# A halved bank, halved merges and stores in the last block, and a new order of all work, in an attention-plus-gated-FFN kernel

## The chip, the core and the metric

The kernel runs on one core of one Trainium2 chip. The metric is the device time of one execution in microseconds (us), lower is better. A core has TensorE (PE: matmuls, with its weight loads listed apart as PEld), VectorE (DVE), ScalarE (ACT), GpSimd (POOL) and SyncE (SP); each of them works through its own list of instructions in order, and they meet through semaphores. Matmuls write into PSUM, which is used here as eight banks of 128 partitions by 512 fp32 numbers; everything else lives in SBUF. DMAs are issued by POOL (all loads) and by SP (transposes and stores).

## The reference

Two layers follow each other. First comes attention with projected keys and values, for 8 batches, 8 heads, 1024 positions and head size 64:

```
k_proj = einsum('ks,bhsd->bhkd', E, k);  v_proj = einsum('ks,bhsd->bhkd', F, v)     # 1024 -> 64
scores = (q @ k_proj^T) / 8;  attn = softmax(scores)
x = (attn @ v_proj), heads side by side, as 8192 tokens of 512
```

Then a gated feed-forward layer, 512 to 1536 and back to 512:

```
out = (sigmoid(x @ w_gate) * (x @ w_val)) @ w_out          # fp32, 8192 x 512
```

## The kernel before

**Blocks.** Each batch has two blocks of 512 tokens, so there are 16 blocks. In a block, three groups of hidden columns are made from x by w_gate and w_val, gated (`tanh` on ACT, `hidden` on DVE), kept as `hT`, and multiplied by w_out. Attention for the next batch runs between the blocks of the present one. Its steps are `kv` (projection), `sc` (scores), `top`, `sub`, `exp` (softmax), `turnp` (a DMA transpose), `xo` (attn times v), `inv`, `ko`, `div` (normalisation) and `turnx` (a DMA transpose to x).

**Seven products.** Apart from block 0, each of the three weight products is done in 2x2 quarters by seven quarter products and not by eight. The sums of quarters that this needs are made in SBUF (`xs`, `s_sum`, `w_sum`, `o_sum`, most through line 547), and the results are put together through three PSUM banks called a, c and f. In the output product (`o_jobs`) bank a gathers A11·B11, S2·T2, A21·T3 and A22·T4. ACT copies it to bank c after the first (`copyO`) and snaps it to SBUF buffers u2 and u3 after the second and third (`snapO`, half scale). Bank c adds A12·B21 and leaves as one quarter of the output (`leaveO`, ACT). Bank f is the shared sum: it takes S1·T1, and DVE merges it with u3 into the quarter (second tokens, second columns); then A12·B22 is added to it, and DVE merges it with u2 into the quarter (first tokens, second columns). A merge is one `scalar_tensor_tensor` of 128x512 (line 1361). The quarter left over comes from bank a at its end. A21 and A12 are overwritten in place by sums; the fourth sum (`sum4`) makes the A12 of the last product.

A quarter product covers 256 tokens, in two halves j of 128 tokens, and writes half j of the bank with 6 matmuls of 128x256. So each half is a job on PE, and a merge waits until both halves are in.

**Stores.** `ost` holds a block's output as four tiles tt of 128 tokens by 512 columns. A quarter is two of those tiles by 256 columns. When both columns' quarters of a tile are there, SP stores the tile (`store`, line 1259, 256 KB), four stores in a block.

**Order.** Nothing schedules at run time. The program first lists all jobs (2911), and then puts them down in the order of the tuple `ORDER`, which so decides the order on every engine at once. `PLACES` says which of the eight banks or thirteen buffers each temporary gets. Waits are derived from the keys that jobs read and write; a bank is one key, so PE's next write into any part of it waits for the readers of all of it. Entries -2 and -1 in `ORDER` are fillers: matmuls of the identity, 512 or 256 columns wide, into bank 7, whose result nobody reads (`busy`). There are 28, all in the first 23 us, while the first inputs land. Then follow the first batch in finer steps (`pk`, `tk`, `tq`, `sc`, `sub`, `pv`, `tp`, `xo0`) and block 0 with plain products (`plainG`, `plainV`).

Of the kernel before, what the change touches and what calls it, by code (L numbers as in the profile page):

```python
# [153 lines left out]
class Job:  # L154
# [222 lines left out]
def bass_linformer_attn__then__ffn_glu_sigmoid_kernel(  # L377
# [11 lines left out]
    B = q.shape[0]  # L389
# [4 lines left out]
    H6 = NF // 2  # L394
# [3 lines left out]
    with contextlib.ExitStack() as es:  # L398
# [103 lines left out]
        def new_bank(**kw):  # L502
            return Slot("bank", group[0], **kw)
# [1373 lines left out]
```

## Time and profile before

| | us |
|---|---|
| median of 3 runs (517.55 to 518.54) | 518.04 |
| the profiled execution | 517.57 |
| its span, first to last instruction | 515.6 |
| last matmul ends, from the span's start | 511.57 |
| PE busy | 509.4 (99%) |
| DVE busy | 443.7 (86%) |
| ACT busy | 371.5 (72%) |
| POOL busy | 173.2 (34%) |

The prediction takes durations from the one profiled execution. Places in time are counted from its span's start. A row of a group is: line, engine, operation, output <- inputs, form, count, then busy time, mean of one in ns, and idle time before. In the timeline a row is: start, length, engine, line, operation, operands, form, count. A matmul's length contains its way through the array, so rows on PE overlap; how densely PE works is read from the distance between starts, which for a 256-column matmul in steady work is 109 ns and for 512 columns 215 ns. The clock granted to TensorE was full throughout (1.000).

### The profile page before, as it was taken

Reading aid. Unit: us, or ns where it says so; the run is one execution under the profiler, and the core shown is the slowest. Engines: PE = TensorE matmul, PEld = TensorE weight load, DVE = VectorE, ACT = ScalarE, POOL = GpSimd, SP = SyncE. Lnnn points to the kernel's source line nnn. Section 1 sums busy time; section 2 is a strip of 40 time slices with the busy share of each in tenths; the row PEclk is TensorE's granted clock in tenths of the full one; section 3 lists DMA queues with packets and bytes.
Section 4 is the critical chain, followed back from the end, with each engine's and each line's share of the span. In section 5 each row is a group of like instructions: output and inputs, shape, how many; then the busy total and the mean of one; then the engine's idle time right before and its main releaser. Section 6 shows DMA issues by size and latency. Waiting matters only on the chain.

```text
span 515.6 us, 12673 instructions
## 1 busy us (share of the span) xinstructions
PE 509.4 (99%) x4975; PEld 420.6 (82%) x4978; DVE 443.7 (86%) x856; ACT 371.5 (72%) x714; POOL 173.2 (34%) x200
## 2 busy tenths in 40 slices
PE   8999999999999999999999999999999999999996
PEld 4556858888888888887888888888888878888885
DVE  6779998499987997889997998989988899977993
ACT  1556866878788587857977777786888669677762
POOL 9975003702435024240354206341163301440020
PEclk9999999999999999999999999999999999999999
DMA  9999958899888248993699937989467953341004
GB/s 167 197 198 207 179 101 181 120 180 223 135 172 147 52 135 123 216 158 88 127 192 183 166 73 143 180 149 139 129 122 175 165 114 76 69 123 61 24 1 164
DMA packets 140411, 71.60 MB, mean 139 GB/s; under 512 B 97216, under 2 KB 132032, under 8 KB 140352
## 3 DMA queue, kind: packets, MB, share of 16 engines
q0 software_dynamic: 35936, 29.89, 38.6%
q1 hardware_dynamic: 104416, 40.91, 37.9%
q8 instruction: 39, 0.64, 0.5%
q14 instruction: 20, 0.16, 0.1%
HBM read 60.29 MB, written 16.78 MB: 149 GB/s over the span
## 4 chain that ended last, share of the span: by engine, by line
PE 96%; DVE 3%; ACT 0%; issue 0%; DVEq 0%
PE pA L518 49%; PE pF L518 47%; DVE topf L1589 1%; DVE hT L1173 1%; DVE spare L1104 0%; DVE pF L1616 0%; DVE pA L1616 0%; DVE hT L547 0%; ACT spare L532 0%; DVE ost L1361 0%; DVE inv L1681 0%; ACT EFT L532 0%; ACT eT L532 0%; DVE KVs L1698 0%; DVE warm L646 0%
## 5 line engine op out<-in xcount | busy, mean ns | idle before, releaser
L532 ACT ACTIVATE spare<-pF 128x512 f32<-128x512 f32 (+2 forms) x157 | 87.4, 574 | 34.9 <-PE pF L518 23.4
L532 ACT ACTIVATE spare<-pA 128x512 f32<-128x512 f32 (+2 forms) x160 | 90.8, 583 | 26.7 <-PE pA L518 18.1
L547 POOL TENSOR_TENSOR hT<-hT,hS 128x512 bf16<-128x512 bf16 x42 | 48.2, 1161 | 131.5 <-PE pA L518 76.5
L1698 POOL TENSOR_TENSOR KVs<-spare,inv 128x256 bf16<-128x256 f32 (+1 forms) x48 | 34.7, 731 | 66.8 <-ACT spare L532 18.4
L1173 DVE SCALAR_TENSOR_TENSOR hT<-spare,pA 128x512 bf16<-128x512 f32 x65 | 43.7, 679 | 10.2 <-PE pF L518 6.1
L532 ACT ACTIVATE spare<-spare 128x512 f32<-128x512 f32 x79 | 48.2, 628 | 5.5 <-DVE spare L1104 5.2
L1104 DVE TENSOR_TENSOR spare<-pA,spare 128x512 f32<-128x512 f32 x62 | 42.0, 682 | 9.6 <-PE pF L518 4.2
L518 PE MATMUL pF<-wO,hT 128*128 128x256 bf16 (+1 forms) x321 | 46.9, 288 | 0.2
L1104 DVE TENSOR_TENSOR spare<-pF,spare 128x512 f32<-128x512 f32 x57 | 38.5, 681 | 3.8 <-PE pF L518 2.1
L1173 DVE SCALAR_TENSOR_TENSOR hT<-spare,pF 128x512 bf16<-128x512 f32 x53 | 35.9, 679 | 4.9 <-PE pF L518 3.4
L518 PEld LDWEIGHTS pF<-wO,hT 128*128 128x128 bf16 x324 | 31.2, 98 | 8.2 <-ACT pF L532 0.2
L518 PE MATMUL pA<-xT,wG 128*128 128x256 bf16 (+1 forms) x216 | 35.1, 284 | 0.0
L518 PE MATMUL pA<-wO,hT 128*128 128x256 bf16 x264 | 34.4, 273 | 0.0
L518 PE MATMUL pA<-xT,wV 128*128 128x256 bf16 (+1 forms) x212 | 34.4, 285 | 0.0
L518 PE MATMUL pA<-wT,hT 128*128 128x256 bf16 x240 | 32.3, 273 | 0.0
L518 PE MATMUL pF<-xT,wV 128*128 128x256 bf16 (+1 forms) x196 | 32.1, 286 | 0.0
L518 PE MATMUL pF<-xT,wG 128*128 128x256 bf16 (+1 forms) x192 | 31.5, 286 | 0.0
L518 PE MATMUL pF<-xS,tV 128*128 128x256 bf16 x200 | 30.0, 273 | 0.0
L518 PEld LDWEIGHTS pA<-wO,hT 128*128 128x128 bf16 x264 | 25.4, 98 | 3.2 <-issue 0.2
L547 POOL TENSOR_TENSOR xS<-xT,xS 128x512 bf16<-128x512 bf16 x14 | 16.9, 1207 | 32.5 <-DVE xS L547 27.5
L518 PE MATMUL pA<-xS,wV 128*128 128x256 bf16 x184 | 27.6, 273 | 0.0
L518 PE MATMUL pA<-xS,tG 128*128 128x256 bf16 x184 | 27.6, 272 | 0.0
(185 smaller groups left out, 1305.7 us busy)
## 6 DMA issues: line engine op xcount, KB each, us to landing
out_dram<-ost SPq DMA_DIRECT2D x64, 256.0 KB, 2.5
KVs<-in_v_dram POOLq DMA_DIRECT2D x15, 512.0 KB, 9.8
KVs<-in_k_dram POOLq DMA_DIRECT2D x14, 512.0 KB, 8.5
Qb<-in_q_dram POOLq DMA_DIRECT2D x14, 512.0 KB, 7.9
wO<-in_moe_w_out_dram POOLq DMA_DIRECT2D x1, 1536.0 KB, 16.6
KVs<-in_k_dram POOLq DMA_DIRECT2D x4, 256.0 KB, 6.2
Qb<-in_q_dram POOLq DMA_DIRECT2D x4, 256.0 KB, 9.5
wG<-in_moe_w_gate_dram POOLq DMA_DIRECT2D x4, 256.0 KB, 11.5
```

The costliest lines, as they stand in the source:

```text
L518: lambda e: e.matmul(o, lhsT, rhs, **kw),
L532: lambda e: e.activation(o, i, func, scale=scale),
L547: fn = lambda e: e.tensor_tensor(o, a, b, op)
L1104: lambda e: e.tensor_tensor(PB(b)[:, :] if stay else BF(s), PB(b)[:, :], BF(s), ALU.add),
L1173: lambda e: e.scalar_tensor_tensor(o, y.rearrange("p (j c) -> p j c", j=2), 1.0, x.rearrange("p (j c) -> p j c", j=2), ALU.add, ALU.mult,),
L1589: lambda e: e.tensor_reduce((top if by_pe(b, t, y) else topf)[:, n : n + 8], PB(bk)[:, :].rearrange("p (n k) -> p n k", n=8), mybir.AxisLi ...
L1698: fn = lambda e: e.tensor_tensor(xto.rearrange("p (g h d) -> p h g d", g=2, h=H)[:, hh[0] : hh[1], :, :], o[:, :, 0:DH].rearrange("p (h g) ...
```

## The change

Three things change together.

1. In the output product of the last block alone, the shared sum f gets a bank for each half j, each started and closed on its own (`own`). The two merges become two each, 128x256, and each waits for its half.
2. The last block's four stores of 256 KB become eight of 128 KB (`store_half`), one for each tile and half of its columns, each of which waits for its own quarter (or half merge).
3. `ORDER` and `PLACES` are new for the whole program, with 2917 jobs, 907 temporaries and 26 fillers (20 of 512 columns, 6 of 256) in place of 2911, 906 and 28 (25 and 3). All other work is the same, instruction for instruction; only its order, its banks and its buffers differ.

```diff
 ORDER = (
-    16, -2, -2, -2, 17, 18, 0, 19, -2, -2, -2, -1, 30, 20, 31, 2, 28, 21, 29, 4, -2, -2, -2, -2, -1, 32, 38, 1,
...
-        def o_product(blk, bk, A, B, j, start=False, stop=False):
+        def o_product(blk, bk, A, B, j, start=False, stop=False, own=False):
...
-                    start=start and m == 0 and j == 0,
-                    stop=stop and m == H6 - 1 and j == 1,
+                    start=start and m == 0 and (own or j == 0),
+                    stop=stop and m == H6 - 1 and (own or j == 1),
...
+        def store_half(blk, tt, col):
+            t = 2 * (2 * (blk % 2) + tt % 2) + tt // 2
+            cc = slice(256 * col, 256 * col + 256)
+            add(
+                "SP",
+                lambda e: e.dma_start(out_v[blk // 2, t][:, cc], ost[:, tt, cc]),
+                r=[("ost", tt, col)],
+                dma=f"out{tt}",
+                cost=0.4,
+                nbytes=128 << 10,
+            )
...
-            a, c, f = new_bank(), new_bank(clean=True), new_bank()
+            last = blk == 2 * B - 1
+            a, c = new_bank(), new_bank(clean=True)
+            f = [new_bank(), new_bank()] if last else [new_bank()] * 2
...
-                        lambda j=j: o_product(blk, b, A, B, j, **kw),
+                        lambda j=j: o_product(blk, b[j] if b is f else b, A, B, j, own=last and b is f, **kw),
...
-                            o,
-                            PB(f)[:, :].rearrange("p (j c) -> p j c", j=2),
+                            o[:, jj, :],
+                            PB(f[jj.start])[:, k].rearrange("p (j c) -> p j c", c=256),
                             0.5,
-                            BF(s).rearrange("p (j c) -> p j c", j=2),
+                            BF(s)[:, k].rearrange("p (j c) -> p j c", c=256),
...
-                job("DVE", pos + step * i + AT["dmerge"], body, name="mergeO")
+                for jj in (slice(0, 1), slice(1, 2)) if last else (slice(0, 2),):
+                    job("DVE", pos + step * i + AT["dmerge"], lambda jj=jj: body(jj), name="mergeO")
...
-            for tt in (2, 3, 0, 1):
+            for tt in () if last else (2, 3, 0, 1):
                 job("SP", pos + step * (5 if tt > 1 else 6), lambda tt=tt: store(blk, tt), name="store")
+            for i, tok, col in ((4, 1, 1), (4, 0, 0), (5, 1, 0), (6, 0, 1)) if last else ():
+                for tt in (2 * tok, 2 * tok + 1):
+                    job("SP", pos + step * i, lambda tt=tt, col=col: store_half(blk, tt, col), name="store")
```

At the end of the new order the instructions stand as follows. On PE, with the last five jobs as before: A12·B21 for j = 1 (bank c), A22·T4 for j = 0 and 1 (bank a), A12·B22 for j = 0 and 1 (bank f). On DVE: the two half merges with u3 (j = 1 first), `sum4`, the half merge with u2 for j = 0, then for j = 1. On SP: the stores of the second columns of tiles 3 and 2, of the first columns of tiles 1 and 0, of tiles 3 and 2, then the second columns of tile 0 and of tile 1.

At the start of the new order the loads up to the first two weight pieces are issued as before. After them POOL issues wG3 (second half), wV3, wG3 (first halves), wG0, wV0 (second halves), Q (head half 1), wV3 (second half), two `norm` jobs, Q (head half 0), wG2, wG1, wG4. Before, Q (head half 0) came ahead of them, wG1 stood between the two `norm` jobs, and wG4 right behind them.

More of the change, by code (lines that the diff above doesn't have):

```diff
@@ L1357, in merge, with body @@
             def merge(i, s, tok, col):
-                def body():
+                def body(jj):
                     o, keys = quarter(tok, col)
+                    k = slice(256 * jj.start, 256 * jj.stop)
                     dve(
                         lambda e: e.scalar_tensor_tensor(
-                            o,
-                            PB(f)[:, :].rearrange("p (j c) -> p j c", j=2),
+                            o[:, jj, :],
+                            PB(f[jj.start])[:, k].rearrange("p (j c) -> p j c", c=256),
                             0.5,
-                            BF(s).rearrange("p (j c) -> p j c", j=2),
+                            BF(s)[:, k].rearrange("p (j c) -> p j c", c=256),
                             ALU.mult,
@@ L1369, in body @@
                         [bf_(s)],
-                        keys,
-                        b=f,
-                    )
-                job("DVE", pos + step * i + AT["dmerge"], body, name="mergeO")
+                        keys[jj],
+                        b=f[jj.start],
+                        n=256 * (jj.stop - jj.start),
+                    )
+                for jj in (slice(0, 1), slice(1, 2)) if last else (slice(0, 2),):
+                    job("DVE", pos + step * i + AT["dmerge"], lambda jj=jj: body(jj), name="mergeO")
             def s_jobs(n, p, cuts=((0, 4), (4, 6))):
```

361 rows, old and new, of tables (ORDER, PLACES) are left out of this document.

## The prediction

> **What bounds the kernel now.** I read the page first (busy time by engine, the chain that ended last), then the waits of PE, the windows of the saturated part, the timeline of the end, and last the identity matmuls of the beginning.
>
> ```profile
> span 515.6 us, 12673 instructions
> PE   509.4 (99%) x4975; PEld 420.6 (82%) x4978; DVE 443.7 (86%) x856; ACT 371.5 (72%) x714; POOL 173.2 (34%) x200
> PE 96%; DVE 3%; ACT 0%; issue 0%; DVEq 0%
> ```
>
> PE is busy 99% of the span, and the chain that ended last lies on PE for 96%. So an instruction on another engine counts only where PE waits for it, or behind the last matmul.
>
> ```profile
> PE pA L518 <- DVE tV L647: 1.1, 1, 1.1
> PE pF L518 <- ACT EFT L532: 0.3, 1, 0.3
> PE pF L518 <- ACT spare L532: 0.2, 1, 0.2
> ```
>
> Those are all the waits of PE that the view of waits names: two at the start and one at 372 us. A matmul's listed length hides short ones, so I also compared starts. From 79 us to the end there are 15 places, without a change of tile form, where the next matmul starts over 60 ns late. Together they make 2.2 us (measured from start to start in the trace). The largest is two in a row at 138 us:
>
> ```profile
> 137.87 0.82 PE L518 MATMUL pA<-wT,hS 128*128 128x256 bf16 x6
> 138.83 0.34 PE L518 MATMUL pF<-vpD,eT 128*128 128x130 bf16 x3
> 139.23 0.35 PE L518 MATMUL pA<-vpD,eT 128*128 128x130 bf16 x3
> ```
>
> Six matmuls 109 ns apart end their turn at 138.52, and the next starts at 138.83: 0.3 us lost. Seven of the 15 places are beside such `xo` rows.
>
> The start holds fillers:
>
> ```profile
> L518 PE MATMUL pA<-ident x28: 272/379/390, 8.2 to 22.6; 128*128 128x512 bf16 x25, 128*128 128x256 bf16 x3
> ```
>
> At the distances that rows show (215.5 ns for 512 columns, 109 for 256) they take 25 x 0.2155 + 3 x 0.109 = 5.71 us of PE's first 23 us.
>
> The end, from the timeline and from windows:
>
> ```profile
> 508.43 0.69 DVE L1361 SCALAR_TENSOR_TENSOR ost<-pA,spare 128x512 f32<-128x512 f32 x1 [2.33 <-PE pA L518]
> ...
> 509.06 0.96 DVE L547 TENSOR_TENSOR hT<-hT,hS 128x1536 bf16<-128x1536 bf16 x1
> ...
> 510.09 1.47 PE L518 MATMUL pA<-wO,hT 128*128 128x256 bf16 x12
> 510.38 0.60 ACT L532 ACTIVATE ost<-pF 128x512 f32<-128x512 f32 x1 [2.04 <-PE pF L518]
> 510.87 0.59 ACT L532 ACTIVATE ost<-pA 128x512 f32<-128x512 f32 x1
> 511.70 0.69 DVE L1361 SCALAR_TENSOR_TENSOR ost<-pA,EF 128x512 f32<-128x512 f32 x1 [1.69 <-PE pA L518]
> ```
>
> ```profile
> 512.84 0.43 SPq L1259 DMA_DIRECT2D out_dram<-ost  x1
> ```
>
> ```profile
> 512.00:512.50 0.50, 0.00 (x0) 0.00 (x0) 0.40 (x1) 0.00 (x0) 0.00 (x0) 1.00 1.07 410
> ```
>
> The last matmul ends at 511.57. The last merge runs 511.70 to 512.40; behind it SP issues two stores, at 512.47 and 512.84. The second lands 2.29 us after its issue, at 515.13, and 0.47 us of closing work follow. A store alone (issued 511.00) lands after 2.03. At 410 GB/s 256 KB take 0.64 us and 128 KB 0.32.
>
> **The change part by part**, against the profiled execution's own 517.57 us, which is 0.47 below the median of 518.04.
>
> *Last merge and stores.* The last merge is half as wide. No row shows that form. DVE takes 0.683 for 512 columns of PSUM, 0.548 for 384 (the division) and 0.422 for 256 (a scaled copy), so I take 0.42; its ends are 0.34 (half of the whole) and 0.69 (no shorter). It starts as before, 0.13 behind the last matmul, and the store of its tile is no longer second in a pair: issue at 511.70 + 0.42 + 0.07 = 512.19 where it was 512.84. SP is free by then: the two stores behind the last `leaveO` (ends 510.98) go at 511.00 and 511.37 as now, and the one for j = 0 follows at 511.85 (its merge ended at 511.46). From issue to landing I take 1.77: the lone 2.03 less half of a transfer, 0.32, plus 0.06, since a row of 1 KB should pay part of its fixed time twice. Landing 513.96 in place of 515.13: **-1.17**. Ends: -1.3 (a half merge of 0.34 and no loss per row) and -0.2 (1 KB rows take as long as 2 KB rows: then four half stores from 511.84 on need 4 x 0.66 us and the last lands near 514.95).
>
> *Two half merges ahead of `sum4`.* The first matmul of the last product at 510.09 comes 0.07 behind the end of `sum4` (509.06 + 0.96); so that chain has nothing to spare. Ahead of it on DVE now stand two merges of 0.42, which overlap by some 0.05: 0.79 for 0.69. **+0.10**, with ends 0 (0.34 twice) and 0.69 (0.69 twice). Queued behind it are the last 12 matmuls, hence all.
>
> *The other merge of this block, its bank, its eight stores.* The product that opens the last use of f no longer waits for a merge of the whole bank; PE did not wait there. The first four half stores are issued between 508.9 and 510.5 (0.33 to 0.44 each), when SP has nothing else. Nothing, unless SP is still busy at 511.0, which would cost up to one issue, 0.4.
>
> *Fillers.* 20 x 0.2155 + 6 x 0.109 = 4.96 us, 0.75 less. That is a gain only if real work can come earlier. In the new order the first `plainV` stands after 10.08 us of other real work on PE, where the first `plainG` now stands after 10.31, at 23.02. Up to it the new list is 0.97 us shorter, so 22.05, with 0.23 more left behind it: -0.74. What must be there: x of `xo0` (two copies of 0.6 behind a matmul row that I place at 19.9, so 21.0) and the first wV piece (issued 8.74, landed 12.2 later, 20.99; now used at 23.45). The tightest load is wG1. It was issued at 16.6 and landed 10.9 later, 27.4; now two loads that land 1.3 us apart stand ahead of it, so 30.1, with its first matmul near 30.9. All loads keep some 0.8 us. **-0.7**; ends -0.75 (the fillers themselves) and 0 (each filler turns into a wait).
>
> *The new order from 60 us on.* PE's work there is the same; what can change is how often it waits. From the written orders I counted the jobs on PE whose round trip (matmul, copy or sum elsewhere by its row's duration, matmul) has under 0.15 us to spare: 38 before and 46 after, from 65 us of PE's work on; under 0.3 us, 73 and 81. 2.2 x 46 / 38 = 2.7: **+0.4**. Its ends: -2.2 (no such wait left) and +2.2 (twice as many). DVE and ACT do the same work in it, at 85% and 75%.
>
> Sum: 517.57 - 1.17 + 0.10 - 0.7 + 0.4 = 516.2 in the execution profiled, and **516.7** against the median.
>
> *A rule against splitting.* In the lines above each of the two stores of a pair has its own latency, and they land 0.6 us apart: latency overlaps, bytes do not. The Trainium skill, "DMA: Bandwidth & Descriptors", "Rules for kernel authors", says to coalesce small transfers into one large one, and its "Anatomy of one DMA" gives 2.0 us plus bytes over 436 GB/s for each. By that, 256 KB would take 2.60 and 128 KB 2.30, an estimate from the page; the trace has 2.03 and 2.29 for 256 KB. With the page's difference of 0.30, and not 0.52, the sum would be 516.9.
>
> **The rivals.**
>
> *Half stores move no faster.* 1 KB rows take as long as 2 KB rows. For it: loads, with rows of 0.5 to 1 KB, move at 200 GB/s in the first 50 us, stores at 410. Against it: those loads also convert types. The end then gives 0.2 and not 1.17: 517.7.
>
> *Fillers become waits.* The softmax chain of the first tiles, not PE, sets the pace up to 23 us. For it: fillers are there because PE had nothing. Against it: real work stands up to 1 us earlier in the new list, and the loads allow it. 516.7 + 0.7 = 517.4.
>
> *The attention rounds wait, and it is slower.* Each `xo` bank is read by `inv` on DVE and `ko` on ACT before its next use. The seven places at `xo` cost 1.44 us together, 0.2 each, out of 84 groups of `xo` after the first batch. For it: ACT's and DVE's queues decide it, and both were reordered throughout. Against it: the jobs with little to spare are about as many. It decides from 12 more such places on: 12 x 0.2 = 2.4 us eat the 1.3 gained and 0.2% more (519.1). At 20 places it gives 516.7 + 4.0 = 520.7.
>
> *The middle gets smoother.* Most of the 2.2 us of late starts go: 516.7 - 0.4 - 1.6 = 514.7.
>
> **How the numbers follow.** 0.2% is 1.04 us, about what a measurement of this kernel can tell from no change; so faster means under 517.0, and slower over 519.1. The forecast has 0.52, with some 0.8 us to either side from the middle: 0.34 of that lies under 517.0, 0.17 within 0.2%, 0.01 above. Half stores no faster has 0.10 and fillers to waits 0.12; of these 0.18 ends within 0.2% and 0.04, with a calmer middle, under 517.0. Attention waits: 0.17, of which 0.15 slower. Smoother: 0.09. Faster: 0.34 + 0.04 + 0.09 = 0.47; same 0.17 + 0.18 + 0.02 = 0.37; slower 0.16. The range for 8 in 10 goes from 515.2 to 519.3; the forecast's own is 515.9 to 517.5.
>
> **What would show it.** Right: the last merge at 0.42 us; last landing about 2.4 us behind the last matmul, where it is 3.56; the first `plain` matmul near 22.05; late starts of 2 to 3 us from 79 us on. Wrong: a wait row of PE above 1 us in the middle; a matmul row that starts late beside `xo`; the first `plain` row still at 23.0; the half stores' packets at less than 300 GB/s.

## The result, and the profile after

The changed kernel takes 516.16 us (median of 7 runs, 515.61 to 516.80), beside 517.55 for the kernel before on the same chip (7 runs, 517.29 to 518.54). The ratio is 0.9971, with a 95% interval from 0.9959 to 0.9983: faster by 0.3%. The execution that was profiled takes 516.16.

The page of the changed kernel, first its span and PE's busy time, then the chain that ended last by engine, then the fillers from the view of the identity tile:

```profile
span 514.4 us, 12647 instructions
PE   508.6 (99%) x4973; PEld 419.1 (81%) x4976; DVE 441.1 (86%) x858; ACT 372.7 (72%) x714; POOL 174.2 (34%) x200
PE 98%; DVE 0%; ACT 0%; issue 0%; DVEq 0%
```

```profile
L518 PE MATMUL pA<-ident x26: 272/379/390, 7.8 to 21.6; 128*128 128x512 bf16 x20, 128*128 128x256 bf16 x6
```

PE is still busy 99% of the span, now 1.2 us shorter (1.23 in the trace). The view of waits names PE's waits:

```profile
PE pA L518 <- DVE tV L647: 1.1, 1, 1.1
PE pF L518 <- DVE hT L1173: 0.4, 1, 0.4
PE pA L518 <- ACT qT L532: 0.4, 1, 0.4
PE pF L518 <- ACT EFT L532: 0.3, 1, 0.3
```

Two of them are new: one for `hT` at 97 us and one for the copy of `qT` at 30 us. The end, from the timeline (all engines, then SP's queue), and the window that was quoted of before:

```profile
508.00 0.76 DVE L1376 SCALAR_TENSOR_TENSOR ost<-pF,spare 128x256 f32<-128x256 f32 x2 [1.64 <-PE pF L518]
...
508.75 0.96 DVE L547 TENSOR_TENSOR hT<-hT,hS 128x1536 bf16<-128x1536 bf16 x1
...
509.79 1.47 PE L518 MATMUL pF<-wO,hT 128*128 128x256 bf16 x12
...
510.72 0.42 DVE L1376 SCALAR_TENSOR_TENSOR ost<-pF,EF 128x256 f32<-128x256 f32 x1 [1.01 <-PE pF L518]
511.37 0.42 DVE L1376 SCALAR_TENSOR_TENSOR ost<-pF,EF 128x256 f32<-128x256 f32 x1 [0.23 <-PE pF L518]
```

```profile
511.55 0.46 SPq L1271 DMA_DIRECT2D out_dram<-ost  x1
512.05 0.45 SPq L1271 DMA_DIRECT2D out_dram<-ost  x1
```

```profile
512.00:512.50 0.50, 0.00 (x0) 0.00 (x0) 0.00 (x0) 0.00 (x0) 0.00 (x0) 1.00 0.75 262
```

The last matmul ends at 511.27, 0.30 earlier than before. Behind it the last merge takes 0.42, SP issues the last store at 512.05, and it lands 1.85 later, at 513.90. From the last matmul to the last landing it is now 2.63 us, where it was 3.56. So 0.93 of the 1.23 us come from the end and 0.30 from everything ahead of it. The profiled time itself fell by 1.41; the 0.18 outside the span (1.97 before, 1.79 now) is not explained by any row.

**Where PE gained and lost its 0.30.** I added up PE's work at the distances that its rows show, without fillers, and compared when equal amounts of it were done. The difference, before minus changed, is called the lead below. In us, at times of the kernel before, for three executions of the changed kernel (two of them from experiments) and the two experiments that hold one part of the change each:

| execution | 8 us | 24 us | 34 us | 86 us | 106 us | 199 us | 219 us | 260 us | 280 us | last matmul |
|---|---|---|---|---|---|---|---|---|---|---|
| changed | 0.46 | 1.02 | 0.47 | 0.45 | -0.15 | 0.53 | 0.63 | 0.68 | 0.32 | 0.30 |
| e3, changed | 0.45 | 0.71 | 0.16 | 0.14 | -0.36 | 0.32 | 0.42 | 0.47 | 0.32 | 0.31 |
| e12, changed | 0.12 | 0.68 | 0.13 | 0.11 | -0.36 | 0.32 | 0.42 | 0.47 | 0.32 | 0.30 |
| e2, new order, old end | 0.43 | 0.99 | 0.44 | 0.42 | -0.23 | 0.45 | -0.09 | -0.05 | -0.20 | -0.21 |
| e1, old order, new end | 0.16 | 0.14 | 0.14 | 0.14 | 0.14 | 0.00 | -0.01 | 0.00 | 0.00 | -0.01 |

Four things are to be read in it. By 24 us the new beginning is 0.7 to 1.0 ahead, of which 0.12 to 0.46 was there at 8 us, before a changed instruction had run. At 30 us it loses 0.55 in every execution. Between 86 and 106 us it loses 0.47 to 0.65 more, at the wait for `hT`, and between 106 and 199 us it gets 0.68 back: the places at 138 us that were late before are not there now. And the chance differences of the beginning are gone at the end in these three executions of the changed kernel (0.12 to 0.46 at 8 us, 0.30 to 0.31 at the last matmul): part of them goes by 24 us, part at 97 and at 273 us. That is not so everywhere: e5 and e6, which keep the changed kernel's order up to the tail, end their last matmul 0.62 and 0.45 ahead of the kernel before. So a lead of 0.3 us at the last matmul can be chance.

The loss at 30 us, from PE's timeline of the changed kernel:

```profile
28.93 0.61 PE L518 MATMUL pA<-ident,Qb 128*128 128x128 bf16 x8
29.37 0.59 PE L518 MATMUL pF<-xT,wV 128*128 128x512 bf16 x2
30.36 0.38 PE L518 MATMUL pA<-kpD,qT 128*128 128x128 bf16 x4 [0.39 <-ACT qT L532]
```

The turns of q (`tq`, first row) are copied by ACT and DVE to `qT`, and the scores product (`sc`, third row) reads that. Only one plain product of 0.43 us stands between the two, and the scores would have been due at 29.80. In the kernel before, two plain products stood there, and nothing waited:

```profile
29.51 0.61 PE L518 MATMUL pF<-ident,Qb 128*128 128x128 bf16 x8
29.96 0.59 PE L518 MATMUL pA<-xT,wV 128*128 128x512 bf16 x2
30.39 0.59 PE L518 MATMUL pF<-xT,wV 128*128 128x512 bf16 x2
30.82 0.39 PE L518 MATMUL pF<-kpD,qT 128*128 128x128 bf16 x4
```

The loss at 97 us, from the timeline of the changed kernel:

```profile
97.00 0.42 DVE L547 TENSOR_TENSOR xS<-xT 128x512 bf16<-128x512 bf16 x1 [3.12 <-DMA xT<-KVs]
97.06 0.60 PE L518 MATMUL pA<-xS,tV 128*128 128x256 bf16 x4
97.35 0.68 DVE L1173 SCALAR_TENSOR_TENSOR hT<-spare,pF 128x512 bf16<-128x512 f32 x1
...
98.08 0.61 PE L518 MATMUL pF<-xS,wG 128*128 128x256 bf16 x4 [0.42 <-DVE hT L1173]
```

DVE stands still for 3.12 us ahead of a sum of x (`xS`), whose input comes by a transposing DMA. The `hidden` (third row) behind it in DVE's list needs nothing from that DMA, and PE's next matmul waits for this `hidden`. Nothing of this shows in DVE's share of 86%.

### The profile page after: what moved, and what is told of

Same layout as the page of the kernel before. It is cut to its first block, busy times and chain, and to the rows that moved or that the text cites. A ratio compares the mean times of both kernels' runs of the same rounds, so it can differ in the third digit from the quotient of the medians.

```text
span 514.4 us, 12647 instructions
## 1 busy us (share of the span) xinstructions
PE 508.6 (99%) x4973; PEld 419.1 (81%) x4976; DVE 441.1 (86%) x858; ACT 372.7 (72%) x714; POOL 174.2 (34%) x200
## 4 chain that ended last, share of the span: by engine, by line
PE 98%; DVE 0%; ACT 0%; issue 0%; DVEq 0%
PE pA L518 51%; PE pF L518 48%; DVE hT L1173 0%; ACT EFT L532 0%; ACT spare L532 0%; ACT qT L532 0%; DVE ost L1376 0%; DVE warm L646 0%; DVE spare L1104 0%; DVE tV L647 0%; DVEq L129 0%
## 5 line engine op out<-in xcount | busy, mean ns | idle before, releaser
L532 ACT ACTIVATE spare<-pA 128x512 f32<-128x512 f32 (+2 forms) x169 | 95.7, 581 | 34.5 <-PE pA L518 22.5
L1718 POOL TENSOR_TENSOR KVs<-spare,inv 128x384 bf16<-128x384 f32 (+1 forms) x51 | 37.9, 751 | 77.5 <-ACT spare L532 16.2
L1173 DVE SCALAR_TENSOR_TENSOR hT<-spare,pA 128x512 bf16<-128x512 f32 x57 | 38.6, 680 | 10.0 <-PE pA L518 8.7
L518 PE MATMUL pA<-xT,wG 128*128 128x256 bf16 (+1 forms) x256 | 41.7, 286 | 0.0
L518 PE MATMUL pA<-wO,hT 128*128 128x256 bf16 (+1 forms) x275 | 37.1, 277 | 0.1
L1104 DVE TENSOR_TENSOR spare<-pF,spare 128x512 f32<-128x512 f32 x50 | 33.9, 682 | 2.7 <-PE pA L518 1.3
L559 POOL DMA_DIRECT2D Qb<-in_q_dram x18 | 14.2, 787 | 49.5 <-ACT ost L532 22.9
L518 PEld LDWEIGHTS pA<-xT,wG 128*128 128x128 bf16 x256 | 24.6, 98 | 6.1 <-ACT pA L532 0.3
L518 PE MATMUL pA<-xS,wG 128*128 128x256 bf16 x192 | 28.7, 273 | 0.0
L518 PE MATMUL pF<-wT,hT 128*128 128x256 bf16 x216 | 28.7, 273 | 0.0
```

Of the source, the lines that this page charges most:

```text
L518: lambda e: e.matmul(o, lhsT, rhs, **kw),
L532: lambda e: e.activation(o, i, func, scale=scale),
L559: add("POOL", lambda e: e.dma_start(o, i), r=r, w=w, dma=sem, cost=0.78, nbytes=nbytes)
L1104: lambda e: e.tensor_tensor(PB(b)[:, :] if stay else BF(s), PB(b)[:, :], BF(s), ALU.add),
L1173: lambda e: e.scalar_tensor_tensor(o, y.rearrange("p (j c) -> p j c", j=2), 1.0, x.rearrange("p (j c) -> p j c", j=2), ALU.add, ALU.mult,),
L1718: fn = lambda e: e.tensor_tensor(xto.rearrange("p (g h d) -> p h g d", g=2, h=H)[:, hh[0] : hh[1], :, :], o[:, :, 0:DH].rearrange("p (h g) ...
```

## The experiments

Experiments sent together ran on one chip beside the same runs of the kernel before. e1 to e4 were one group (before 517.54, 35 runs), e5 to e8 another (517.75, 19 runs), e9 to e12 the third (517.95, 15 runs).

### e1 to e4: the parts, one by one

e1 has the old order, banks and fillers with the new end; only the tail of the list differs from the kernel before:

```diff
-    2876, 2893, 2874, 2895, 2884, 2894, 2877, 2883, 2888, 2878, 2897, 2898, 2896, 2899, 2889, 2900, 2901, 2890,
-    2902, 2904, 2903, 2905, 2891, 2908, 2907, 2906, 2909, 2910,
+    2876, 2893, 2874, 2895, 2884, 2894, 2877, 2883, 2888, 2878, 2897, 2898, 2896, 2899, 2889, 2901, 2900, 2902,
+    2910, 2891, 2890, 2909, 2903, 2912, 2905, 2911, 2904, 2906, 2907, 2914, 2913, 2908, 2915, 2916,
```

> The old order and banks with the new end alone: own bank for each half of the last shared sum, half merges, half stores, and the last twelve matmul jobs' companions in the new order's places. Theory by steps (the end is worth 0.9 to 1.1 us, and the order only the rest): last landing 2.6 us behind the last matmul in place of 3.56, time 0.9 to 1.1 us under the kernel before, ratio 0.9980, and the last matmul where the kernel before has it, 511.5, apart from what the first 8 us do by chance. Rival (the order carries the gain, and the end was hidden anyway): 0 to 0.3 us, ratio 0.9995 or more.

e2 has the new order with the old end (one bank f, whole merges, four stores):

```diff
-    2884, 2877, 2883, 2895, 2878, 2894, 2812, 2896, 2780, 2897, 2898, 2888, 2899, 2889, 2901, 2900, 2902, 2910,
-    2891, 2890, 2909, 2903, 2912, 2905, 2911, 2904, 2906, 2907, 2914, 2913, 2908, 2915, 2916,
+    2884, 2877, 2883, 2895, 2878, 2894, 2812, 2896, 2780, 2897, 2898, 2888, 2899, 2889, 2900, 2901, 2891, 2890,
+    2902, 2904, 2903, 2905, 2908, 2907, 2906, 2909, 2910,
...
-            f = [new_bank(), new_bank()] if last else [new_bank()] * 2
+            a, c, f = new_bank(), new_bank(clean=True), new_bank()
```

> The new order, banks, buffers and fillers with the old end: one bank for the shared sum, whole merges, four whole stores. Theory by steps: last landing 3.5 us behind the last matmul; time 0.3 to 0.5 us under the kernel before, ratio 0.9992, of which the fillers hold nothing, because the 0.55 us that PE is ahead at 28 us are lost at the wait for qT at 30 us. Rival (the order carries the gain): 1.0 to 1.4 us, ratio 0.9975.

e3 is the changed kernel itself on this chip.

> The changed kernel once more, beside the two halves of the change. If the first 8 us differ by chance from execution to execution, its first projection matmul starts anywhere from 7.2 to 7.7 us here, and so do those of the other runs, whose instructions up to there are the same; if the new order makes them earlier, it starts at 7.2 here and in the run with the order alone, and at 7.7 in the run with the end alone. Time as measured before: ratio 0.996 to 0.998.

e4 is the changed kernel without its 26 fillers (every -2 and -1 taken out of `ORDER`):

```diff
-    16, -2, -2, -2, 17, 18, 4, 19, -2, -2, -2, -1, 28, 20, 29, 1, 30, 21, 31, -2, -1, 22, 0, 32, 2, 38, 33, -2,
+    16, 17, 18, 4, 19, 28, 20, 29, 1, 30, 21, 31, 22, 0, 32, 2, 38, 33,
```

> The changed kernel without any of its 26 fillers (4.96 us of PE work less, nothing else differs). If the fillers only stand where PE waits anyway, the first plain matmul comes at most 0.3 us earlier and the time is the changed kernel's within 0.3 us. If fillers delay real work, it is up to 1 us faster. If they keep PE's matmuls at full rate (the first fp32 transposes stand 213 ns apart and then 110), rows in the first 25 us get longer without them, 256 columns at twice their 109 ns in part, and the time is 1 to 4 us longer.

| run | median us (runs) | ratio to before, 95% interval | last matmul to last landing |
|---|---|---|---|
| e1, new end alone | 516.70 (11) | 0.9982 [0.9974, 0.9991] | 2.63 |
| e2, new order alone | 517.13 (11) | 0.9995 [0.9987, 1.0004] | 3.51 |
| e3, both | 516.50 (11) | 0.9985 [0.9974, 0.9996] | 2.64 |
| e4, both without fillers | 517.29 (12) | 0.9991 [0.9978, 1.0004] | 2.63 |

The new end alone gives 0.84 us of time (517.54 less 516.70; 0.9 to 1.1 was expected), and its gap from the last matmul to the last landing is the changed kernel's 2.63. The last matmul ends at 511.60, where it was 511.57. So the end is worth 0.9 wherever it stands, and the other banks and the merges ahead of `sum4` cost at most those 0.03.

The new order alone gives 0.41 by the medians, but its interval reaches over 1, and on top of the new end it gives 0.20 (516.70 less 516.50), within the scatter of these runs: no experiment of this group shows by its time that the order is worth anything. The two parts come to 1.25 one by one, both together to 1.04. The profiled execution of e2 shows one thing that can take the order's gain away. From PE's timeline of e2:

```profile
217.14 0.60 PE L517 MATMUL pA<-xS,wG 128*128 128x256 bf16 x4
218.21 0.61 PE L517 MATMUL pA<-xT,wG 128*128 128x256 bf16 x4 [0.47 <-DMA xT<-KVs]
```

PE waits here for a transposing DMA to x. The profiled execution of the changed kernel has no wait at this place. There are two of these transposes. In the trace the second is issued at 209.94 in the changed kernel and at 210.02 in e2, but lands 5.7 us later in the one (215.63) and 8.2 later in the other (218.16), with PE due near 217.6. Ahead of them lies a load of q that the new order issues at 206.5, where it was 201.4 before. That load lands at 212.29 in the changed kernel and at 214.90 in e2, and the first transposes land 2.57 and 2.49 behind it. Over all twelve executions of the new order that have a trace, the load takes 5.7 to 6.2 us in eight and 8.2 to 8.7 in four (e2, e4, e10 and e12), and the transposes land 2.5 to 2.6 behind it in ten and 1.0 to 1.2 in two. PE waits at this place in three of the four with the slow load. In the kernel before, this load had landed at 208.99, and the second transposes took 4.2. That load and transposes share the way is what this suggests; I did not test it by moving the load, and what makes the load slow is open.

e4 answers for the fillers only in part. In its profiled execution PE is 1.3 us behind the changed kernel's at 24 us. From PE's timeline of e4, and the same two pieces of work in the changed kernel:

```profile
11.52 1.06 PE L517 MATMUL pA<-KVs,EFT 128*64 128x256 bf16 x8 [0.28 <-DMA KVs<-in_k_dram]
12.52 1.03 PE L517 MATMUL pA<-kpD,qT 128*128 128x128 bf16 x8
```

```profile
11.04 0.63 PE L518 MATMUL pA<-KVs,EFT 128*64 128x256 bf16 x8
11.60 0.62 PE L518 MATMUL pA<-kpD,qT 128*128 128x128 bf16 x8
```

The same matmuls take 1.06 and 1.03 us for 0.63 and 0.62. The granted clock fell to one half in this execution, from 10.80 to 14.22 us (the windows of e4 ahead of the fall and during it; the column behind POOL is the clock):

```profile
7.39:10.80 3.41, 1.46 (x22) 0.92 (x19) 1.47 (x4) 0.00 (x0) 3.41 (x6) 1.00 1.43 188
10.80:14.22 3.42, 3.14 (x30) 2.02 (x27) 1.59 (x4) 0.00 (x0) 3.42 (x6) 0.50 1.39 201
```

In the 3.41 us ahead of the fall PE was busy for 1.46; with the fillers it is busy for all of them in the changed kernel, and the clock there is 1.00. So a filler can do more than pass the time: where PE rested for more than half of 3.4 us here, its clock was at half for the next 3.4. The Trainium skill, "TensorE: Matmul & The Clock Gate", "Part 1: The HAM clock gate", tells of a clock that falls to half when the array was idle for a window and comes back after a busy one. These rows agree with the half and with the return behind 3.14 busy us of 3.42; but the stretch ahead of the fall was not idle, it held 1.46 us of work.

What the fillers are worth is not shown by this. The profiled execution took 518.85 us, the second longest of the twelve, and its mean clock was 0.996; three of the twelve have a mean clock of 0.996 or 0.997, the other nine 0.999 or 1.000, at 515.37 to 517.63 us. So the fall of the clock does not explain the 0.79 us between the medians of e4 and e3, the lowest time of e4 is under every run of e3 (516.12 to 519.26), and the two intervals overlap. Whether the fillers gain anything in a usual execution stays open.

### e5 and e6: which half does it

e5 keeps the half banks and half merges, and stores whole tiles:

```diff
-            for tt in () if last else (2, 3, 0, 1):
+            for tt in (2, 3, 0, 1):
...
-            for i, tok, col in ((4, 1, 1), (4, 0, 0), (5, 1, 0), (6, 0, 1)) if last else ():
-                for tt in (2 * tok, 2 * tok + 1):
-                    job("SP", pos + step * i, lambda tt=tt, col=col: store_half(blk, tt, col), name="store")
```

> The changed kernel with its half banks and half merges, but with four whole stores of 256 KB in place of the eight halves. The figure to read is the gap from the end of the last matmul to the last landing: 3.56 us before, 2.63 changed. Theory A (the half merge sets when the last pair may be issued, the size of the store sets issue to landing, and each gives a part): the last half merge ends 0.53 behind the last matmul as in the changed kernel, the two last issues begin 0.07 and 0.44 later, and the second lands 2.29 behind its issue as before: gap 0.53 + 0.07 + 0.37 + 2.29 = 3.26 us, time 0.6 us over the changed kernel. Theory B (the merges give it all, the size of a store is nothing): gap 2.6 to 2.8, time as the changed kernel.

e6 keeps the eight half stores, with one bank and whole merges:

```diff
-            f = [new_bank(), new_bank()] if last else [new_bank()] * 2
+            f = [new_bank()] * 2
...
-                for jj in (slice(0, 1), slice(1, 2)) if last else (slice(0, 2),):
+                for jj in (slice(0, 2),):
```

> The changed kernel with its eight half stores, but with one bank and whole merges of 0.69 us. Theory A: the last merge ends 0.82 behind the last matmul as before, the two last issues begin about 0.08 and 0.55 later, and the second lands 1.85 behind its issue: gap 0.82 + 0.55 + 1.85 = 3.2 us, 0.6 over the changed kernel. Theory B (the half merges do it): gap 3.5, as before. Theory C (the size of the stores does it all): gap 2.6 to 2.7, time as the changed kernel.

The gap is 3.36 us in e5 and 3.06 in e6; 3.56 before, 2.63 with both. The times are 517.23 (11 runs, 0.9989 [0.9980, 0.9999]) and 516.73 (8 runs, 0.9987 [0.9974, 0.9999]). Theory A holds for the gap: each alone gives a part, 0.20 and 0.50. Together they give 0.93, which is 0.23 more than the two parts. The times do not decide: the changed kernel was not in this group, and the 1.02 us that e6 gains on the kernel before lie near its own gains in the other groups (1.04 to 1.58). From SP's queue and DVE in the timeline, e5 first, e6 second:

```profile
511.05 0.42 DVE L1376 SCALAR_TENSOR_TENSOR ost<-pF,EF 128x256 f32<-128x256 f32 x1 [0.23 <-PE pF L518]
511.23 0.96 SPq L1259 DMA_DIRECT2D out_dram<-ost  x2
```

```profile
511.25 0.69 DVE L1375 SCALAR_TENSOR_TENSOR ost<-pF,EF 128x512 f32<-128x512 f32 x1 [1.69 <-DMA out_dram<-ost]
512.34 0.43 SPq L1270 DMA_DIRECT2D out_dram<-ost  x1
```

In e5 the merge is done at 511.48, 0.53 behind the last matmul. But SP has issued four whole stores one right behind the other (at 510.38, 510.75, 511.23 and 511.73), and they take 2.04, 2.30, 2.55 and 2.58 us to land. The last issue stands 0.78 behind the last matmul, where it was 1.28 before; but the last store lands 2.58 behind its issue and not 2.28, so the queue of 256 KB transfers takes back 0.30 of the 0.50. In e6 the merge ends 0.83 behind the last matmul as before, and the last half store lands 1.83 behind its issue. With both, the half stores hardly queue (1.71, 1.85, 1.78, 1.92, 1.69, 1.83, 1.88 and 1.85 from issue to landing) and so the early merge pays.

### e7 to e12: the two new waits

e7 moves the scores product (job 86) behind the next two turns of q:

```diff
-    144, 133, 82, 143, 362, 85, 83, 150, 145, 86, 195, 102, 104, 87, 92, 105, 152, 93, 103, 199, 88, 156, 154,
+    144, 133, 82, 143, 362, 85, 83, 150, 145, 195, 102, 104, 86, 87, 92, 105, 152, 93, 103, 199, 88, 156, 154,
```

> The changed kernel with one job (the scores product that waits for the copy of qT at 30 us) moved behind the next plain product and one more projection, so that two jobs of 0.43 us stand ahead of it and not one. Theory A: the wait of 0.55 us at 30 us goes, the lead of 0.55 over the changed kernel is kept to the last matmul, and the time falls by about 0.5 us. Rival D: the order is tight enough that a later wait takes the gain back (the one at 97 us for a transposing DMA, or the one at 273 us for a sum on POOL, where a lead of 0.2 was lost between two executions of the changed kernel): lead 0.5 at 60 us, under 0.15 at the last matmul, time as the changed kernel.

It gained next to nothing: the lead over the changed kernel went from -0.31 to -0.24 across 30 us, and the time is 516.44 (6 runs, 0.9971 [0.9960, 0.9983]). Neither theory had the reason. PE's timeline of e7:

```profile
29.69 0.59 PE L518 MATMUL pF<-xT,wV 128*128 128x512 bf16 x2
30.59 0.38 PE L518 MATMUL pA<-ident,Qb 128*128 128x128 bf16 x4 [0.32 <-DVE qT L755]
```

Now the next turns wait, for the DVE copy of the same `qT`: their bank comes free only when that copy has read it. The wait hangs on the copies, not on who asks for them.

e8 moves the sum that stands still at 97 us (job 437) behind the `hidden` that PE waits for (job 470), five entries further down:

```diff
-    433, 455, 468, 417, 519, 534, 471, 558, 520, 453, 536, 469, 456, 521, 437, 416, 454, 522, 458, 415, 470,
+    433, 455, 468, 417, 519, 534, 471, 558, 520, 453, 536, 469, 456, 521, 416, 454, 522, 458, 415, 470, 437,
```

> The changed kernel with one VectorE sum (xS from xT, which stands still 3.12 us for a transposing DMA at 97 us) moved behind the sum hidden that PE waits for. Theory A: PE's wait of 0.59 us at 97.5 us goes, the time falls by 0.5 to 0.6 us. Rival D: PE meets the late xS a little later instead, or loses the gain at 138 or 273 us: lead over the changed kernel under 0.15 at the last matmul, time as the changed kernel.

The wait is gone. The timeline of e8 has `hidden` at 96.22 and the same matmuls of `xS` and wG at 97.41, which follow those at 96.98 without a break:

```profile
96.22 0.69 DVE L1173 SCALAR_TENSOR_TENSOR hT<-spare,pF 128x512 bf16<-128x512 f32 x1 [2.42 <-ACT spare L532]
...
96.98 0.60 PE L518 MATMUL pA<-xS,tV 128*128 128x256 bf16 x4
...
97.41 0.60 PE L518 MATMUL pF<-xS,wG 128*128 128x256 bf16 x4
```

The lead over the changed kernel rises by 0.60 there, falls by 0.17 at 102 us, where PE's next weights then wait 0.27 for a sum on DVE, and 0.43 is left at 106 us and stays until 260 us. (At the last matmul it is 0.72, but only because the changed kernel's own profiled execution loses 0.36 us around 273 us, where all the others, e4 apart, lose 0.15. This 0.2 is in every lead over it from there on.) The time is 516.10 (5 runs, 0.9963 [0.9949, 0.9976]).

e9 goes at the copies at 30 us: the turns of q (84 and 82) stand one plain product earlier, ACT's copy (85) ahead of a tanh (144), DVE's copy (83) ahead of a gate (133):

```diff
-    81, 194, 147, 128, 136, 15, 146, 196, 148, 140, 130, 198, 137, 132, 149, 138, 131, 13, 142, 139, 184, 84,
-    144, 133, 82, 143, 362, 85, 83, 150, 145, 86, 195, 102, 104, 87, 92, 105, 152, 93, 103, 199, 88, 156, 154,
+    81, 194, 147, 128, 136, 15, 146, 196, 148, 140, 130, 198, 137, 132, 149, 138, 131, 13, 139, 184, 84, 82,
+    142, 143, 362, 85, 144, 83, 133, 150, 145, 86, 195, 102, 104, 87, 92, 105, 152, 93, 103, 199, 88, 156, 154,
```

> The changed kernel with the two turns of q (tq) at 29 us one plain product earlier on PE, the copy of qT by ACT ahead of a tanh, and the copy by VectorE ahead of a gate. Moving the scores product back had left the wait where it was (the next turns then waited 0.32 us for the same copy of qT to free their bank). Theory A (the round trip turn, copy, scores is simply 0.55 us too short of cover): the lead over the changed kernel rises by 0.45 to 0.55 between 25 and 35 us, stays so until 95 us, and the time falls by 0.3 to 0.5 us. Rival D (the copies, tanh and gates stand in each other's way at that place whatever their order): a new wait between 29 and 34 us, the lead rises by less than 0.15, the time is that of the changed kernel.

e10 has both moves, e11 is e8 again, and e12 the changed kernel again.

> Both moves, the turns of q of the run before it and the sum behind hidden. Theory A (the two waits are separate): lead over the changed kernel at the last matmul 0.9, time 0.7 to 0.9 us under the changed kernel and about 2 under the kernel before. Rival D (the transposing DMA at 97 us does not come earlier with PE, so the lead of 30 us is lost there): lead 0.4 to 0.5 at the last matmul, time as with the second move alone.

> The kernel with the sum moved behind hidden once more, beside the changed kernel on one chip. It had kept a lead of 0.43 us of the 0.59 at 97 us (0.17 went at 102 us, where PE then waited for a VectorE sum). If that is so, the time is 0.3 to 0.5 us under the changed kernel; if the 0.35 between the medians of two calls was scatter, the intervals lie over each other with a difference under 0.2.

> The changed kernel itself for the comparison on one chip: 516.2 to 516.8 us, gap from the last matmul to the last landing 2.63 us, the waits at 30 us (0.55) and 97 us (0.4 to 0.6) as before.

| run | median us (runs, lowest to highest) | ratio to before, 95% interval | lead over changed at 34 / 106 / 199 / 219 us, last matmul |
|---|---|---|---|
| e12, changed | 516.37 (8, 515.77 to 516.94) | 0.9967 [0.9955, 0.9979] | -0.34 / -0.20 / -0.21 / -0.20, 0.00 |
| e9, turns earlier | 515.75 (6, 515.60 to 516.19) | 0.9956 [0.9941, 0.9971] | 0.30 / 0.23 / 0.22 / 0.22, 0.43 |
| e11, `hidden` first | 515.93 (6, 515.63 to 517.05) | 0.9961 [0.9946, 0.9976] | -0.27 / 0.05 / 0.04 / 0.04, 0.25 |
| e10, both | 516.03 (8, 515.10 to 516.93) | 0.9961 [0.9947, 0.9975] | 0.14 / 0.35 / 0.35 / -0.69, -0.50 |

The wait at 30 us is gone in e9, as PE's timeline of it shows: turns, two plain products, scores, each right behind the other.

```profile
28.70 0.61 PE L518 MATMUL pA<-ident,Qb 128*128 128x128 bf16 x8
29.15 0.59 PE L518 MATMUL pA<-xT,wG 128*128 128x512 bf16 x2
29.58 0.59 PE L518 MATMUL pF<-xT,wV 128*128 128x512 bf16 x2
30.01 0.39 PE L518 MATMUL pA<-kpD,qT 128*128 128x128 bf16 x4
```

In e9 the lead over the changed kernel rises there by 0.50 (-0.20 to 0.30); 0.24 of it is lost again near 40 us, where the expectation had it stay, and the rest stays. The median is 0.62 under the changed kernel on the same chip, of which the profiled executions of the two show 0.43 at the last matmul.

e11 has the wait at 97 us gone as e8 has, and its median is 0.44 under the changed kernel, where 0.3 to 0.5 was expected. But that does not confirm a worth of 0.44: its six runs (515.63 to 517.05) lie over the eight of e12, and its lead over e12 at the last matmul is 0.25, less than the 0.32 by which e5 leads e12 without any change ahead of the tail. Against the kernel before, an execution without the move loses 0.25 to 0.64 us between 94 and 106 us (eight of them, e4 left out), one with it still 0.18 to 0.39 (e8, e11 and e10), because PE is then late at 102 us. So the move takes this wait away, and what that is worth is some 0.2 us by the traces.

The two moves together did not add up in the profiled execution: 0.54 more at 30 us and 0.60 at 97 us, but then 0.39 lost at 102 us and 1.04 at 218 us, there at the transposing DMA that e2 had met. PE's timeline of e10:

```profile
216.71 0.60 PE L518 MATMUL pA<-xS,wG 128*128 128x256 bf16 x4
218.18 0.61 PE L518 MATMUL pA<-xT,wG 128*128 128x256 bf16 x4 [0.87 <-DMA xT<-KVs]
```

Its transposes land at 217.37 and 218.13, behind a load of q that took 8.7 us and landed at 214.82. The lowest two of its eight runs, 515.10 and 515.14, are the lowest of the group; whether these are the ones without that wait can't be seen, since only one execution has a trace. So e9 most likely beats the changed kernel (their intervals against the kernel before lie over each other, but the highest of its six times, 516.19, is under the changed kernel's median); whether e10 does better than e9 stays open until the load of q at 206 us stands earlier.

## Why the prediction was right

The sum was 516.7, with faster as the likeliest outcome, and 516.16 is inside the forecast's own range. The sum was 1.3 us under the median of 518.04 that it started from; measured side by side, the medians lie 1.39 us apart here, 1.04 in the group of e3 and 1.58 in that of e12. By its steps:

- **Last merge and stores, -1.17: the mechanism was right, the size 0.24 too big.** The end gave 0.93. The half merge takes 0.42 as taken. Two sizes were off. SP was not free: an issue of a half store takes 0.45 us where several follow each other, and the one for j = 0 ran from 511.55 to 512.01, so the last issue was 0.25 behind its merge and not 0.07 (511.80 to 512.05). And the half store lands 1.85 behind its issue, not 1.77, since it is second in a pair; alone it takes 1.70.
- **Two half merges ahead of `sum4`, +0.10: right in kind, 0.03 in size.** They take 0.76 (0.79 was taken). In e1, with the order of before, `sum4` starts at 509.11 where it was 509.06, and the last matmul ends 0.03 later.
- **The other merge, its bank and its stores, 0: right** for PE; SP being busy is the 0.18 above.
- **Fillers, -0.7: right at the place, and then given back.** The first plain matmul stands at 21.78 in the profiled execution and at 22.09 and 22.12 in e3 and e12, where 22.05 was predicted. By 24 us the lead is 0.7 to 1.0, part of it chance from the first 8 us. But I checked the round trips of the new order only from 65 us on. The round trip of q at 30 us lies ahead of that, is covered by one plain product where two stood, and takes 0.55 back in all executions. e9 puts the cover back and gets 0.50, of which 0.26 lasts beyond 40 us.
- **The new order from 60 us on, +0.4: too much.** Counted as the prediction counts them, the late starts from 79 us on are 15 with 2.22 us before, and 19 with 2.53, 18 with 2.20 and 18 with 2.19 us in three executions of the changed kernel: +0.31, -0.02 and -0.03. The count of tight round trips did not say which of them would wait. The largest new one, 0.46 to 0.59 at 97 us, is no round trip of PE at all: it is a sum that waits for a DMA with the wanted job queued behind it.

So the two failed steps, 0.55 missing and 0.4 too much, cancelled by luck, and the total is better than its parts. The beginning of the profiled execution was lucky besides: 0.46 us ahead at 8 us, before a changed instruction had run.

Of the rivals, *half stores move no faster* falls: the gap shrank, and e6 shows 0.50 for the size of the stores alone. In the trace a packet of 1 KB takes 44 to 46 ns and one of 2 KB 84, which on 16 engines is some 360 and 390 GB/s (an estimate); the 262 of the window shown above has the engines busy for a share of 0.75 only. *Fillers become waits* names the right place, the beginning, but not the right wait: PE did come earlier to its plain work. *The attention rounds wait* did not occur: late starts beside `xo` are five with 0.49 us in the changed kernel, where they were seven with 1.43. *The middle gets smoother* names that rightly, but new late starts elsewhere take it back.

The rule to coalesce small transfers (the Trainium skill, "DMA: Bandwidth & Descriptors", "Rules for kernel authors"), taken by itself, speaks for whole stores. Here a whole one takes 2.03 alone and 2.29 as second of a pair, a half one 1.70 and 1.85: 0.33 and 0.44 less, of which the first is near the page's estimate of 0.30 and the second nearer to the 0.52 of the prediction. The page's fit is for DMAs that GpSimd issues, and these stores are issued by SP. At the very end of this kernel, where nothing hides the landing, smaller last transfers were the better choice.

## What to carry to other kernels

When a list of work is written anew, look at the round trips of the beginning as closely as at those of the bulk: work pulled ahead by 0.7 us is worth only what the next dependent product leaves of it. Look also for jobs that wait for a DMA and stand ahead of something PE needs in the same engine's list; moving one such job by five entries took its wait away (worth some 0.2 us by the traces, not settled by the times), and putting two turns and their copies one product earlier lowered the median by 0.62, where the whole change was worth 1.0 to 1.6. For the last bytes of a kernel, try to halve both what is computed last and what is stored last: here either alone gave 0.20 and 0.50, both 0.93. And before a difference of a few tenths is called a gain, see how far two executions of one order lie apart: here up to 0.3 us at the last matmul.

## What the runs showed of the hardware

The first fp32 transposes on PE take 1.61 us in the execution before and 1.14 in the changed kernel, with the same instructions ahead of them (timelines of the two):

```profile
5.81 1.61 PE L518 MATMUL pF<-tV,EF 128*128 128x128 f32 x8
```

```profile
5.76 1.14 PE L518 MATMUL pF<-tV,EF 128*128 128x128 f32 x8
```

In the trace they start 213 ns apart at first in the former and then 110; in the latter they are some 110 apart from the second on. Over all executions the group takes 1.07 to 1.83 us, whatever the kernel. The granted clock in the windows is 1.00 there, but the windows count as full speed what no clock record covers, and the first record of a trace, which is of full speed, begins somewhere from 3.97 to 7.22 us. Where it begins late (6.75 us in e5, 6.94 before, 7.22 in e11), the transposes stand 213 ns apart until just then; in the other eleven executions it begins by 5.79 us, and they stand some 110 apart. So PE starts at half its rate, and when it goes over to the full one differs by up to 3 us from one execution to the next. The full clock that is stated for the kernel before holds from 6.94 us on, and a difference of half a microsecond at 6 us between two profiles is no effect of a change.

Transposing DMAs of one size, at one place of the list, take from 4.2 to 9.1 us from issue to landing, and the load of q ahead of them 5.7 to 8.7. An order that is tight around such a transfer can show it as scatter of the total. The eight runs of e10 lie between 515.10 and 516.93; that their scatter comes from there is not shown.
